# Column maxima of one more batch by GpSimd instead of TensorE, fewer idle products, and a new hand-written order of all pieces

## The chip, the core and the metric

The kernel runs on one core of a Trainium2 chip. The metric is device time in microseconds (us) of one execution, as the median over runs. The engines are PE (TensorE: matrix products and transposes), DVE (VectorE), ACT (ScalarE: functions by table), POOL (GpSimd) and SP (SyncE, which here only issues DMAs, in order). "PEld" is the load of weights into PE, which overlaps its products.

## The reference, cut to what matters

```python
q_s = softmax(q over the 64 elements of a head)       # q, k, v: 8 batches, 8 heads, 576 x 64
k_s = exp(k - max(k over the 576 positions)); k_s /= sum over the positions
kv  = einsum('bhsd,bhse->bhde', k_s, v)
x   = einsum('bhsd,bhde->bhse', q_s, kv)  # then 4608 tokens x 512
h   = x @ w_in                            # 512 -> 2048
g   = softplus(h)
out = g @ w_out                           # 2048 -> 512
```

## The kernel before

The 4608 tokens are nine tiles of 512. A tile's `x` is made from four head pairs h; `h` and `g` are handled in 16 blocks j of 128. Most products run as three fp32r products of a high and a low part (hi·hi, hi·lo, lo·hi; L595 to L597 for the up products, L637 to L639 for the down products), and a 128x512 product of this kind is the unit of nearly all of PE's work. Tiles 0 to 2 are made plainly; tiles 3 to 8 in three pairs by a scheme with seven products in place of eight (L722 to L724, L836 to L838), whose operands are sums of blocks that DVE, ACT and POOL form (L252 to L293, L679 to L686, L803). Weights are decoded and split once in tile 0, stored to DRAM (`keep_w`, L220) and fetched again later (`fetch_w`, L224; `fetch_in`, L230), as are the sums (L265, L293, fetched at L241, L790).

For each batch b and head pair h a "kv unit" of ten pieces makes `kv`: `top` (DVE reduces the five chunks of positions to one maximum for each partition and column, L336), the maximum over the 128 partitions, `shift` (DVE subtracts, L371), `power` (ACT, exp, L377), `product` (PE, L387), and `scale`, `high`, `low`. For the maximum over the partitions there are two ways. Up to batch `ON_PE`, PE transposes the maxima (`turn`, L355), DVE reduces them to a column (`across`, L364) and PE transposes the column, spread to 128 columns, back (`spread`, L367); `shift` reads it from PSUM. Above `ON_PE`, POOL does it in one call (L339) and the pieces 1 to 3 are empty. Batch 0 has a form of its own (L350, L360).

No scheduler orders the work. One string, `ORDER`, names every piece, and `do` issues the pieces one after the other; each engine runs its own instructions in that order, and semaphores hold it where a piece's input isn't there. Tokens: `k2.1.3` is piece 3 of the kv unit of batch 2, head pair 1; `q` softmax of q; `x` a piece of x's making (flip of q, split, product); `T M S J P Q` decoding and splitting of weights; `U A G O` (with 16t+j) up products, softplus, split of g, down products; `D` and `R` stores and fetches; `Y y X C r t e d o` the paired scheme; `n` and `L` loads of k, v and q. `w5.5` issues five idle products of the identity into a bank nobody reads (L1038); they stand at the start, before PE has real work. Batches are 0-based in the code: the "third batch" is b = 2.

Of the kernel before, what the change touches and what calls it, by code (L numbers as in the profile page):

```python
# [1096 lines left out]
```

## Time and profile before

| what | value |
|---|---|
| time, median of 3 runs | 814.32 us (813.33 to 815.51) |
| span of the profiled execution, first to last instruction | 811.1 us |
| median time less this span | 3.2 us |
| PE busy | 800.8 us, 99% of the span |
| DVE, ACT, POOL busy | 625.9, 536.3, 115.1 us |
| granted PE clock | 1.000 |

The profiled execution has no time of its own apart from its span; the 3.2 us between the span and the median are taken as what lies around it. Busy time of PE is counted with overlaps of pipelined products taken once; a 128x512 fp32r product is listed with 0.39 us, but the next one starts 0.23 us after it.

### The profile page before, as it was taken

The numbers are of one execution on the slowest core, as the hardware profiler recorded it, in microseconds if no ns is written. First come the engines' busy times: TensorE is split into PE (matmuls) and PEld (weight loads), VectorE is DVE, ScalarE is ACT, GpSimd is POOL, SyncE is SP. The second block draws the span as 40 slices with busy tenths as digits, with TensorE's granted clock in tenths as the row PEclk, the third lists the DMA queues.
The fourth block names the chain that finished last, engine by engine and source line by source line (L and its number), as shares of the span: only waits on it lengthen the run. The fifth ranks groups of instructions, "written<-read, shape, count | busy, mean of one in ns | idle before, by whom it ended". The sixth has DMA issues, their size and how long they took to land.

```text
span 811.1 us, 12147 instructions
## 1 busy us (share of the span) xinstructions
PE 800.8 (99%) x4244; PEld 656.6 (81%) x4244; DVE 625.9 (77%) x1027; ACT 536.3 (66%) x868; POOL 115.1 (14%) x219
## 2 busy tenths in 40 slices
...
PEclk9999999999999999999999999999999999999999
...
GB/s 340 373 273 182 59 39 274 267 176 385 401 279 257 328 337 343 340 372 253 139 324 237 186 115 265 275 270 93 280 201 197 178 261 198 175 156 322 211 126 70
DMA packets 114493, 193.75 MB, mean 239 GB/s; under 512 B 8000, under 2 KB 90176, under 8 KB 104192
## 3 DMA queue, kind: packets, MB, share of 16 engines
...
q10 hardware_dynamic: 320, 0.26, 0.1%
...
HBM read 149.95 MB, written 42.99 MB: 238 GB/s over the span
## 4 chain that ended last, share of the span: by engine, by line
PE 92%; DVE 3%; issue 2%; DMA 2%; SPq 1%; ACT 0%; POOL 0%; DVEq 0%; ACTq 0%; POOLq 0%
PE po L722 6%; PE po L838 6%; PE po L836 6%; PE po L837 6%; PE po L724 6%; PE po L723 6%; PE ph L595 5%; PE po L637 5%; PE ph L597 5%; PE ph L596 5%; PE po L638 5%; PE po L639 5%; PE ph L722 3%; PE ph L724 3%; PE ph L723 3%; PE ph L836 3%
## 5 line engine op out<-in xcount | busy, mean ns | idle before, releaser
L881 POOL DMA_DIRECT2D out<-w x92 | 59.3, 653 | 305.7 <-DVE w L873 304.4
L816 ACT CAST g_hi<-w 128x512 fp32r<-128x512 f32 x74 | 46.2, 624 | 31.1 <-PE ph L837 8.0
L595 PE MATMUL ph<-x,w 128*128 128x512 f32 x164 | 65.3, 398 | 1.1 <-DMA w<-kept 1.1
L637 PE MATMUL po<-w,g_hi 128*128 128x512 f32 x164 | 64.5, 394 | 0.0
L596 PE MATMUL ph<-x,w 128*128 128x512 f32 x164 | 64.0, 390 | 0.0
L597 PE MATMUL ph<-x,w 128*128 128x512 f32 x164 | 64.0, 390 | 0.0
L639 PE MATMUL po<-w,g_lo 128*128 128x512 f32 x164 | 64.0, 390 | 0.0
L638 PE MATMUL po<-w,g_hi 128*128 128x512 f32 x164 | 63.9, 390 | 0.0
L819 DVE TENSOR_TENSOR g_lo<-w,g_hi 128x512 fp32r<-128x512 f32 x74 | 51.0, 690 | 16.0 <-ACT g_hi L816 12.6
L803 DVE TENSOR_TENSOR w<-w,w 128x512 f32<-128x512 f32 x72 | 49.2, 686 | 5.3 <-ACT w L756 5.2
L752 ACT ACTIVATE w<-w 128x512 f32<-128x512 f32 x48 | 30.1, 632 | 34.8 <-DVE w L745 18.9
L745 DVE TENSOR_TENSOR w<-po,w 128x512 f32<-128x512 f32 x24 | 16.6, 690 | 46.9 <-PE po L724 46.3
L816 ACT CAST w<-w 128x512 fp32r<-128x512 f32 x52 | 32.2, 623 | 25.1 <-DVE w L819 8.1
L604 ACT ACTIVATE g<-ph 128x512 f32<-128x512 f32 x48 | 28.6, 599 | 29.8 <-PE ph L597 26.7
L722 PE MATMUL po<-w,x 128*128 128x512 f32 x112 | 44.1, 394 | 0.0
L724 PE MATMUL po<-w,x 128*128 128x512 f32 x112 | 43.7, 390 | 0.0
L723 PE MATMUL po<-w,x 128*128 128x512 f32 x112 | 43.7, 390 | 0.0
L610 ACT CAST g_hi<-g 128x512 fp32r<-128x512 f32 x46 | 28.6, 621 | 21.2 <-PE po L638 20.7
L613 DVE TENSOR_TENSOR g_lo<-g,g_hi 128x512 fp32r<-128x512 f32 x46 | 31.4, 683 | 12.6 <-ACT g_hi L610 12.4
L339 POOL PARTITION_ALL_REDUCE mx<-mx x20 | 17.2, 860 | 160.6 <-DVE mx L336 133.0
L336 DVE TENSOR_REDUCE mx<-kvt 128x128 f32<-128x640 f32 x28 | 36.9, 1319 | 2.5 <-DMA kvt<-in_kv_tail 2.5
L819 DVE TENSOR_TENSOR w<-w,w 128x512 fp32r<-128x512 f32 x52 | 35.6, 689 | 3.1 <-ACT w L816 1.0
...
## 6 DMA issues: line engine op xcount, KB each, us to landing
...
```

Of the source, the lines that this page charges most:

```text
L595: nc.tensor.matmul(ph, lhsT=w_hi, rhs=x_hi, start=h == 0, stop=False)
L596: nc.tensor.matmul(ph, lhsT=w_lo, rhs=x_hi, start=False, stop=False)
L597: nc.tensor.matmul(ph, lhsT=w_hi, rhs=x_lo, start=False, stop=h == HP - 1)
L637: nc.tensor.matmul(po, lhsT=g_hi[:, ms], rhs=w_hi, start=j == 0, stop=False)
L638: nc.tensor.matmul(po, lhsT=g_hi[:, ms], rhs=w_lo, start=False, stop=False)
L639: nc.tensor.matmul(po, lhsT=g_lo[:, ms], rhs=w_hi, start=False, stop=j == NJ - 1)
L722: nc.tensor.matmul(ph, lhsT=w_hi, rhs=x_hi, start=c == 0 and i in (0, 4), stop=False, **more)
L723: nc.tensor.matmul(ph, lhsT=w_lo, rhs=x_hi, start=False, stop=False, **more)
L724: nc.tensor.matmul(ph, lhsT=w_hi, rhs=x_lo, start=False, stop=c == 1, **more)
L816: nc.scalar.copy(ring[p, i, s][0], right_of(p, i, s))
L819: engine.tensor_tensor(out=lo, in0=right_of(p, i, s), in1=hi.bitcast(F32), op=ALU.subtract)
L836: nc.tensor.matmul(bank, lhsT=w_hi, rhs=hi, start=begin, stop=False, **more)
```

## The change

`ON_PE` goes from 2 to 1, so that the four kv units of batch 2 take their maxima over the partitions from POOL: eight transposes on PE (four L355, four L367) and four short reductions on DVE (L364) go, four calls of L339 come. Of 38 idle products 31 stay, in blocks of 20, 2, 3, 4 and 2 in place of 20, 5, 6 and 7. `ORDER` is written anew from end to end; no other piece is dropped or added (some tokens that did nothing are gone). The functions are the same, 156 lines further down, since the new string is written over many lines. Two ACT table loads fewer follow from the order (48 to 46).

```diff
-ON_PE = 2
+ON_PE = 1
...
 ORDER = """
-    w0.20 b0 b1 q0.0 n k0.0.1 n q0.1 n n q0.2 q0.3 q0.4.1 l0 q0.5 l1 k0.0.2 k0.1.1 l2 k0.1.2 k0.0.3 ...
+    b0 q0.0 b1 q0.1 n n w0.20 k0.0.1 n n q0.2 q0.3 q0.5 q0.4.1 q0.6 k0.0.2 k0.1.1 k0.1.2 k0.0.3 k0.0.4 k0.0.5
+    k0.2.1 k0.2.2 k0.1.3 k0.1.4 w4.2 k0.2.3 k0.2.4 w5.3 k0.1.5 q0.8 l0 k0.3.1 k0.3.2 k0.2.5 k0.0.6 T0 M0.1 w1.2
...
```

**The start, on PE.** Before, the last idle products and the first products of tile 0's x (L558, L583 are its first products of `x` and of `h`):

```order
L480 MATMUL ph_145<-s,pair 128x32
L382 MATMUL att_107<-one,x_192 64x1 x10
L387 MATMUL po_142<-x_192 64x64 x10
L382 MATMUL att_108<-one,x_197 64x1 x10
L387 MATMUL po_143<-x_197 64x64 x10
L1038 MATMUL ph_144<-ident 128x128 x7
L558 MATMUL po_140<-w_137,q_lo 128x512
L558 MATMUL po_141<-w_137,q_lo 128x512
```

After, the same place (156 lines on):

```order
L636 MATMUL ph_145<-s,pair 128x32 x2
L1194 MATMUL ph_144<-ident 128x128 x2
L538 MATMUL att_107<-one,x_192 64x1 x10
L543 MATMUL po_142<-x_192 64x64 x10
L538 MATMUL att_108<-one,x_197 64x1 x10
L543 MATMUL po_143<-x_197 64x64 x10
L714 MATMUL po_141<-w_137,q_lo 128x512
L714 MATMUL po_140<-w_137,q_lo 128x512
```

The seven idle products just ahead of x's first product are gone, two stand further ahead, and x begins with head pair 1 in place of 0.

**Batch 2's transposes, on PE.** Before, amid the down products of tile 0, two of the eight stand here; after, no L511 or L523 (the same two lines) stands behind those of batch 1:

```order
L637 MATMUL po_1387<-w_575,g_hi 128x512
L638 MATMUL po_1387<-w_575,g_hi 128x512
L639 MATMUL po_1387<-w_575,g_lo 128x512
L367 MATMUL att_107<-ident,m_1560 128x128
L355 MATMUL att_108<-ident,mx 128x128
L637 MATMUL po_1384<-w_635,g_hi 128x512
```

**Tile 2's fetches of weights, on SP.** Before, the fetches (L224) for the up products U34 (`w_2120`) and U35 (`w_2180`) stand one pair of loads of k and v (L314, L318) apart:

```order
L265 DMA sums_1963<-w_1682 128x2048
L432 DMA qt<-in_q 128x2048
L224 DMA spare<-kept_1292 128x2048
L265 DMA sums_2037<-w_1711 128x2048
L241 DMA x_2060<-sums_1963 128x2048
L314 DMA kvt<-in_kv 128x8x128
L318 DMA kvt<-in_kv_tail 64x2x128
L224 DMA w_2120<-kept_1309 128x2048
L314 DMA kvt<-in_kv 128x8x128
L318 DMA kvt<-in_kv_tail 64x2x128
L224 DMA w_2180<-kept_1324 128x2048
```

After, with U34's weights in `w_2146` and U35's in `w_2168`:

```order
L421 DMA sums_2046<-w_1248 128x2048
L380 DMA spare<-kept_1586 128x2048
L421 DMA sums_2089<-w_1577 128x2048
L470 DMA kvt<-in_kv 128x8x128
L474 DMA kvt<-in_kv_tail 64x2x128
L380 DMA w_2146<-kept_832 128x2048
L470 DMA kvt<-in_kv 128x8x128
L474 DMA kvt<-in_kv_tail 64x2x128
L380 DMA w_2168<-kept_1075 128x2048
```

The load of q's next tile and the fetch of the sums (L241) stand elsewhere now; the two pairs of loads are still between and ahead of the fetches.

**U34 and U35, on PE.** Before, they follow each other:

```order
L596 MATMUL ph_2205<-x_2054,w_2120 128x512
L597 MATMUL ph_2205<-x_2054,w_2120 128x512
L595 MATMUL ph_2234<-x_1740,w_2180 128x512
L596 MATMUL ph_2234<-x_1740,w_2180 128x512
L597 MATMUL ph_2234<-x_1740,w_2180 128x512
```

After, 24 down products and two groups of products of k and v stand between; the rows at the seam to U35:

```order
L795 MATMUL po_2218<-spare,g_lo 128x512
L543 MATMUL att_107<-kvt 64x65 x10
L543 MATMUL att_108<-kvt 64x65 x10
L751 MATMUL ph_2301<-x_1715,w_2168 128x512
L752 MATMUL ph_2301<-x_1715,w_2168 128x512
```

## Rows read from the trace of the kernel before

**Rows 1.** The page: busy time by engine, granted clock, chain that ended last.
```profile
PE 800.8 (99%) x4244; PEld 656.6 (81%) x4244; DVE 625.9 (77%) x1027; ACT 536.3 (66%) x868; POOL 115.1 (14%) x219
...
PEclk9999999999999999999999999999999999999999
...
PE 92%; DVE 3%; issue 2%; DMA 2%; SPq 1%; ACT 0%; POOL 0%; DVEq 0%; ACTq 0%; POOLq 0%
```

**Rows 2.** Waits of PE: line waited for, total us, times, longest.
```profile
PE ph L595 <- DMA w<-kept: 1.1, 1, 1.1
...
PE att L535 <- DVE q_lo L529: 0.7, 1, 0.7
...
PE att L387 <- issue: 0.4, 1, 0.4
```

**Rows 3.** Busy time in four stretches: window, engines' busy us (count), PEclk, DMA.
```profile
3.00:30.00 27.00, 26.20 (x335) 22.12 (x336) 23.79 (x53) 16.46 (x28) 7.92 (x17) 1.00 1.05 371
30.00:50.00 20.00, 20.00 (x79) 11.09 (x78) 14.51 (x21) 19.91 (x27) 6.07 (x5) 1.00 1.04 388
...
120.00:180.00 60.00, 60.00 (x321) 49.27 (x320) 30.88 (x58) 30.66 (x46) 8.15 (x12) 1.00 0.61 235
...
240.00:280.00 40.00, 39.29 (x241) 32.12 (x238) 39.51 (x71) 27.95 (x48) 4.34 (x15) 1.00 0.85 280
```

**Rows 4.** Timeline of PE around one transpose: start, duration, line, operation.
```profile
127.83 0.27 PE L355 MATMUL att<-ident,mx 128*128 128x128 f32 x1
127.86 0.48 PE L595 MATMUL ph<-x,w 128*128 128x512 f32 x1
128.18 0.39 PE L596 MATMUL ph<-x,w 128*128 128x512 f32 x1
```

**Rows 5.** Timeline of PE and DVE at the start (an fp32 product counts twice).
```profile
2.99 6.07 PE L1038 MATMUL ph<-ident 128*128 128x128 f32 x40 [2.99 <-DVE ident L120]
...
23.77 1.83 PE L1038 MATMUL ph<-ident 128*128 128x128 f32 x14
23.91 1.28 DVE L555 STREAM_TRANSPOSE w<-qt 128x512 f32<-128x512 f32 x2
25.44 3.60 PE L558 MATMUL po<-w,q_lo 128*128 128x512 f32 x8
28.87 1.45 PE L583 MATMUL ph<-x,w 128*128 128x512 f32 x3
```

**Rows 6.** The chain of waits around U35: start, duration, what.
```profile
222.23 2.55 SPq L318
224.82 8.94 DMA w<-kept
...
233.89 0.47 PE ph L595
```

**Rows 7.** Timeline of DVE and PE at 254 us.
```profile
254.39 1.21 DVE L473 TENSOR_REDUCE s<-qt 128x32 f32<-128x1024 f32 x1
255.52 0.68 DVE L529 TENSOR_TENSOR q_lo<-att,q_hi 128x512 fp32r<-128x512 f32 x1
256.25 0.36 PE L535 MATMUL att<-q_hi,kv_hi 128*128 128x192 f32 x1 [0.71 <-DVE q_lo L529]
```

**Rows 8.** POOL's reductions: the line's durations and who waited for them.
```profile
L339 POOL PARTITION_ALL_REDUCE mx<-mx x20: 702/711/1528, 198.0 to 527.5; - x20
...
  DVE kvt L371: 3.8, 6
```

**Rows 9.** One ACT table load and what follows it, timeline of ACT.
```profile
83.37 1.28 ACT L604 ACT_TABLE_LOAD   x1
84.66 0.60 ACT L604 ACTIVATE g<-ph 128x512 f32<-128x512 f32 x1
```

**Rows 10.** The end, timeline of all engines.
```profile
797.94 7.69 POOL L881 DMA_DIRECT2D out<-w  x12 [5.00 <-DVE w L873]
805.74 0.39 PE L838 MATMUL po<-x,spare 128*128 128x512 f32 x1
807.49 1.21 SPq L904 DMA_DIRECT2D out<-w  x2
```

More of the change, by code (lines that the diff above doesn't have):

```diff
@@ new lines @@
+    b0 q0.0 b1 q0.1 n n w0.20 k0.0.1 n n q0.2 q0.3 q0.5 q0.4.1 q0.6 k0.0.2 k0.1.1 k0.1.2 k0.0.3 k0.0.4 k0.0.5
+    k0.2.1 k0.2.2 k0.1.3 k0.1.4 w4.2 k0.2.3 k0.2.4 w5.3 k0.1.5 q0.8 l0 k0.3.1 k0.3.2 k0.2.5 k0.0.6 T0 M0.1 w1.2
+    q0.7 k0.0.7 l1 T1 M1.1 w2.2 k0.3.3 k0.3.4 k0.1.6 k0.3.5 l2 q0.12 k0.1.7 k0.1.8 q0.13 w3.2 q0.9 q0.11.1 q0.10
+    x0.1.0 k0.0.8 l3 n l4 T2 k0.2.6 k0.2.7 k0.2.8 x0.0.0 k0.3.6 k0.3.7 x0.3.0 k0.3.8 x0.1.1 x0.0.1 x0.1.2 x0.2.0
+    J0 k1.0.0 x0.3.1 x0.2.1 x0.0.2 x0.3.2 B0 T3 J1 B1 k1.0.1 x0.2.2 B2 B3 k1.0.2 U0 M2.1 J2 k1.0.3 k1.0.4 n
@@ new lines @@
+    k1.1.0 U1 M3 S3.1 J3 T4 k1.1.1 M4.1 k1.0.5 A0 A1 L1 q1.0 P2 l5.6.7.8.9 k1.0.6 x0.0.3 x0.3.3 Q2 x0.3.4 x0.0.4
+    x0.1.3 x0.1.4 x0.2.3 x0.2.4 P3 Q3 O0 U2 U3 T5 M5 J4 q1.1 T7 k1.1.2 k1.1.3 q1.2 k1.0.7 T6 A2 G2 A3 O1 k1.1.4
+    S5.1 J5 P4 M6.1 Q4 J6 P5 k1.2.0 O2 G3 q1.3 T8 Q5.1 U4 U5 O3 M8.1 M7.1 J7 k1.1.5 k1.1.6 P6 Q6 z1 A4 G4 O4 J8
+    k1.1.7 q1.4 P7 Q7 A5 G5 T11 T10 M10 U6 T9 M9 S10 S9 J9 P8 Q8 A6 G6 U7 A7 O5 D5 U8 q1.5 q1.7 z0 k1.1.8 k1.1.9
+    k1.0.8 k1.0.9 k1.2.1 O6 P9 Q9 D2 k1.2.2 T12 M12.1 k1.3.0 k1.3.1 G7 k1.2.3 q1.6 M11.1 J10 P10 q1.8 J11 O7 A8
@@ new lines @@
+    Q10 T14 P11 Q11 G8 J12 q1.9 U9 W1 U10 A9 U11 T13 P12 A10 A11 O8 G9 O9 M13.1 Q12 D6 k1.3.2 k1.3.3 M14.1
+    k1.2.4 k1.2.5 J13 P13 G10 G11 k1.3.4 Q13 k1.3.5 T15 M15.1 J14 k1.2.6 k1.2.7 k1.2.8 k1.2.9 q1.10 x1.0.0 J15
+    U12 O10 U13 k1.3.6 A12 G12 D3 k1.3.7 x1.0.1 W3 W2 W0 x1.0.2 P14 Q14 O11 O12 x1.0.3 D14 A13 G13 k1.3.8 k1.3.9
+    P15 x1.1.0 x1.1.1 x1.1.2 O13 Q15.1 P0 x1.1.3 q1.11 x1.0.4 x1.0.5 x1.2.0 x1.2.1 U14 U15 x1.2.2 x1.2.3 x1.1.4
+    x1.1.5 A14 G14 x1.3.0 Q0.1 O14 P1 x1.2.4 x1.3.1 x1.3.2 x1.3.3 x1.3.4 k2.0.0 Q1.1 x1.2.5 x1.3.5 Y0.0 k2.1.0
@@ new lines @@
+    k2.1.4 U16 A15 L2 U17 A16 U18 A17 D0 G15 A18 O15 q2.0 k2.0.4 D15 q2.1 q2.2 q2.3 G16 G17 D9 q2.5 q2.7 U19
+    q2.4.1 q2.6 q2.8 O16 G18 O17 k2.0.5 k2.0.6 k2.1.5 q2.9 q2.10 k2.0.7 D8 k2.0.8 k2.0.9 A19 G19 k2.1.6 n k2.2.0
+    O18 U20 U21 A20 A21 U22 U23 k2.2.4 k2.2.5 k2.2.6 O19 k2.1.7 k2.1.8 n k2.3.0 k2.3.4 k2.3.5 q2.11 G20 A22 Y0.1
+    Y1.1 A23 k2.2.7 k2.2.8 D1 Y2.1 Y2.0 Y2.2 O20 U24 U25 Y3.0 G21 Y2.3 Y2.4 k2.1.9 O21 D4 G22 H1.7.0 Y2.5 Y3.1
+    Y0.2 Y0.3 O22 Y0.4 Y0.5 D10 Y0.6 H1.7.1 O23 k2.2.9 x2.0.0 x2.0.1 x2.0.2 x2.0.3 A24 A25 Y3.2 Y3.3 Y1.0 x2.0.4
@@ new lines @@
+    Y3.4 x2.0.5 Y3.5 Y1.2 H1.8.0 H1.9.0 H1.8.1 k2.3.6 k2.3.7 Y2.6 Y4.1 U26 A26 Y2.7 k2.3.8 k2.3.9 O24 H1.9.1 D12
+    O25 n n H1.10.0 x2.1.0 U27 x2.1.1 k3.0.0 x2.1.2 x2.1.3 L3 k3.1.0 Y3.6 q3.1 x2.2.0 H1.10.1 x2.2.1 U28 x2.1.4
+    A27 H1.11.0 Y1.3 Y1.4 Y1.5 A28 O26 H1.12.0 D7 U29 U30 H1.11.1 Y2.8 R0.0 x2.2.2 x2.2.3 x2.1.5 x2.3.0 L4 Y4.0
+    Y7.0 Y4.2 A29 Y7.1 Y4.3 A30 D13 O27 Y6.0 Y3.7 Y3.8 H1.12.1 x2.3.1 Y0.7 k3.0.4 k3.0.5 q3.0 Y6.1 O28 x2.3.2
+    x2.3.3 U31 Y1.6 Y1.7 H1.13.0 H1.13.1 k3.1.4 k3.1.5 H1.14.0 H1.14.1 x2.3.4 x2.3.5 x2.2.4 x2.2.5 q3.12 q3.2
@@ new lines @@
+    q3.4 O29 y0.0 A31 q3.3 H1.15.0 Y0.8 Y7.2 R0.1 k3.0.6 y0.1 y0.2 y0.3 k3.0.7 q3.6 q3.8 q3.5 q3.7 q3.13 q4.0
+    k3.1.6 Y1.8 U32 U33 k3.1.7 A32 O30 H1.15.1 Y4.4 n k3.2.0 R0.2 q3.9 k3.2.4 k3.1.8 n k3.3.0 H2.0.0 q3.11
+    H2.0.1 R0.3 R0.4 O31 F1.0 F1.1 F1.2 k3.1.9 A33 H2.1.0 H2.1.1 q3.10 U34 F1.3 O32 R0.5 y2.0 A34 k3.2.5 H2.2.0
+    k3.3.4 k3.0.8 k3.0.9 q4.1 y1.1 k3.3.5 q4.12 O33 k3.2.6 k3.2.7 H2.2.1 k3.2.8 y1.0 k3.3.6 k3.3.7 k3.3.8 q4.2
+    y0.4 U35 y1.2 q4.4 k3.2.9 y2.1 k3.3.9 y0.5 U36 n A35 H2.3.0 x3.0.0 H2.3.1 q4.6 U37 D11 O34 x3.0.1 q4.3
@@ new lines @@
+    k4.0.0 q4.5 A36 H2.4.0 y0.6 q4.7 x3.0.2 x3.0.3 n x3.1.0 x3.1.1 O35 k4.1.0 q4.8 x3.1.2 x3.1.3 A37 R0.6 U38
+    Y6.2 x3.0.6 x3.2.0 Y7.3 k4.0.4 x3.2.1 k4.1.4 k4.0.5 q4.13 x3.2.2 x3.2.3 x3.1.6 H2.4.1 R0.7 O36 R0.8 x3.2.6
+    x3.3.0 x3.3.1 y0.7 k4.0.6 x3.3.2 Y7.4 y1.3 k4.1.5 k4.0.7 y1.4 x3.3.3 q4.9 q4.11 y1.5 y3.1 A38 H2.5.0 H2.5.1
+    y0.8 k4.0.8 k4.0.9 U39 H2.6.0 H2.6.1 x3.3.6 k4.1.6 k4.1.7 Y4.5 O37 R0.9 n n y1.6 y1.7 A39 H2.7.0 y1.8 y4.0
+    U40 U41 R0.10 Y4.6 Y4.7 Y5.0 Y6.3 Y6.4 Y6.5 Y4.8 k4.2.0 k4.3.0 H2.7.1 k4.1.8 k4.1.9 O38 y3.0 R0.11 A40
@@ new lines @@
+    H2.8.0 Y6.6 H2.8.1 Y6.7 O39 R0.12 O40 y3.2 R0.13 k4.2.4 A41 k4.3.4 H2.9.0 H2.9.1 U42 Y7.5 Y5.2 Y5.1 R2.0
+    k4.3.5 y5.0 Y5.3 Y5.4 y3.3 Y5.5 y3.4 k4.2.5 k4.2.6 k4.3.6 A42 H2.10.0 Y6.8 U43 k4.2.7 k4.2.8 Y5.6 y4.1
+    k4.2.9 X0.1.hB11 q4.10 x4.0.0 k4.3.7 Y7.6 Y7.7 Y7.8 x4.0.1 O41 x4.0.2 k4.3.8 k4.3.9 x4.0.3 x4.1.0 x4.1.1
+    Y5.7 Y5.8 x4.0.6 x4.1.2 U44 x4.2.0 x4.1.3 X0.0.hB11 H2.10.1 x4.2.1 y3.5 X0.0.lB11 x4.1.6 x4.3.0 A43 H2.11.0
+    R0.14 O42 R0.15 x4.2.2 y4.2 x4.2.3 x4.2.6 x4.3.1 X0.1.hB21 X0.0.T1 y5.1 H2.11.1 X0.0.hB22 X0.0.T3 X0.1.lB21
@@ new lines @@
+    A44 x4.3.2 y3.6 y4.3 X0.1.lB11 y3.7 X0.1.T1 X0.0.hT1 y4.4 X0.1.hT1 H2.12.0 U45 O43 y4.5 x4.3.3 X0.0.lB22
+    X0.0.T2 H2.12.1 y4.6 y5.2 y5.3 x4.3.6 X0.0.hB21 X0.0.lB21 X0.0.T4 X0.1.T3 X0.1.hB22 n X0.1.lT1 R3.1.0 A45
+    H2.13.0 X0.1.hT3 U46 A46 O44 U47 y3.8 R3.0.0 R2.1 n X0.1.lB22 y4.7 H2.13.1 y6.0 X0.0.hT2 X0.0.lT2 y4.8 O45
+    X0.1.T2 H2.14.0 H2.14.1 I2.14.0 X0.1.lT3 X0.1.hT2 X0.1.T4 y6.1 X0.0.lT1 R4.1.0 A47 H2.15.0 R4.3.0 H2.15.1
+    I2.14.1 X0.0.hT3 C0.0.0 y7.1 X0.1.hT4 X0.1.lT4 y5.4 y5.5 X0.0.lT3 X0.0.hT4 X0.0.lT4 I2.15.0 C0.0.7 C0.0.2
@@ new lines @@
+    y6.2 X0.1.lT2 y6.3 y6.4 y6.5 R4.0.0 L5 y5.6 y5.7 R3.2.0 L6 C0.0.1 C0.0.8 C0.0.9 y2.2 y2.3 y2.4 I2.15.1 F2.0
+    F2.1 C0.0.3 C0.1.0 F2.2 F2.3 C0.0.4 C0.1.7 k5.0.0 y5.8 C0.1.1 R4.2.0 C0.0.10 C0.0.5 y2.5 C0.0.11 C0.0.6 R2.2
+    C0.1.8 C0.1.3 y2.6 y2.7 y2.8 R4.4.0 C0.1.2 C0.2.0 C0.1.9 y7.0 y7.2 y7.3 y7.4 y7.5 k5.1.0 R3.3.0 C0.1.10 y7.6
+    y7.7 C0.1.4 C0.1.11 C0.0.14 C0.1.5 R2.3 C0.2.7 C0.2.2 C0.2.1 R3.4.0 C0.1.6 k5.0.4 k5.0.5 k5.0.6 R4.5.0 n
+    y6.6 C0.2.8 k5.1.4 k5.1.5 C0.2.9 k5.1.6 C0.0.15 C0.0.16 q5.0 q5.1 q5.12 C0.0.12 C0.2.3 q5.2 C0.2.10 C0.3.0
@@ new lines @@
+    C0.2.4 q5.3 n C0.2.5 R2.4 C0.1.14 C0.3.7 C0.3.1 y6.7 C0.3.2 k5.0.7 k5.1.7 q5.5 k5.1.8 C0.2.11 C0.2.12 C0.3.9
+    y6.8 C0.4.0 C0.2.6 R4.6.0 C0.3.8 C0.3.3 C0.1.15 C0.3.4 R3.5.0 k5.2.0 k5.3.0 C0.2.14 k5.0.8 k5.0.9 C0.3.10
+    C0.3.5 R2.5 k5.2.4 C0.3.11 k5.2.5 C0.3.6 C0.4.7 q5.4 t0.1.0 C0.4.1 k5.3.4 k5.3.5 C0.4.2 R3.6.0 k5.2.6 k5.1.9
+    C0.3.15 q6.0 C0.2.15 C0.4.8 q5.6 q5.7 q5.8 k5.3.6 C0.3.16 k5.2.7 k5.3.7 C0.4.3 q5.13 q5.9 k5.3.8 q5.11
+    C0.4.10 C0.4.4 k5.2.8 C0.3.14 C0.5.0 C0.5.7 C0.5.4 C0.4.11 C0.4.5 C0.4.14 C0.5.2 C0.5.9 e0.0.0.0 C0.5.1
@@ new lines @@
+    t0.1.1 q5.10 k5.2.9 x5.0.0 x5.0.1 x5.0.2 e0.0.0.1 C0.5.8 k5.3.9 C0.4.6 C0.4.9 t0.1.4 e0.0.1.0 e0.0.1.1
+    C0.5.3 C0.5.10 x5.1.0 C0.1.16 C0.5.11 x5.0.3 y7.8 x5.1.1 n x5.1.2 C0.4.15 x5.0.6 C0.6.0 C0.6.7 x5.2.0 n
+    t0.1.3 k6.0.0 k6.1.0 C0.5.5 x5.1.3 C0.1.12 k6.0.4 x5.2.1 R2.6 C0.6.4 C0.6.1 x5.1.6 R3.7.0 C0.4.12 C0.6.8
+    C0.5.6 k6.0.5 C0.6.3 C0.6.10 x5.2.2 C0.7.0 x5.3.0 k6.1.4 k6.1.5 x5.2.3 x5.3.1 C0.6.11 C0.6.5 x5.3.2 C0.5.15
+    C0.5.14 q6.1 x5.2.6 e0.0.3.0 e0.0.3.1 C0.7.7 e0.0.2.0 t0.1.5 e0.0.2.1 q6.12 C0.6.2 x5.3.3 k6.0.6 C0.6.14
@@ new lines @@
+    R2.7 C0.7.1 C0.7.4 q6.2 C0.6.9 q6.3 X1.1.hB11 X1.1.lB11 C0.5.16 C0.6.6 x5.3.6 k6.1.6 C0.7.8 k6.0.7 k6.0.8
+    X1.0.hB11 q6.4 q6.6 q6.5 k6.0.9 r0.0 C0.7.3 C0.7.10 C0.2.16 d0.0.0 n k6.2.0 r0.1 d0.0.1 d0.0.2 q6.8 n R4.7.0
+    C0.7.11 e0.0.4.0 e0.0.5.0 X1.0.lB11 k6.1.7 k6.1.8 t0.1.2 C0.7.5 k6.1.9 r0.2 C0.7.2 r0.3 C0.7.9 e0.0.4.1
+    e0.0.6.0 q6.7 d0.0.3 e0.0.5.1 e0.0.7.0 C0.3.12 d0.0.4 C0.7.6 k6.2.4 e0.0.7.1 d0.0.5 e0.3.0.0 k6.3.0 k6.2.5
+    e0.0.6.1 e0.3.0.1 d0.0.6 d0.0.7 C0.6.12 C0.6.15 d0.3.0 C0.7.15 e0.3.1.0 C0.5.12 k6.2.6 n k6.3.4 k6.3.5
@@ new lines @@
+    k6.3.6 e0.3.3.0 t0.2.0 t0.3.0 r0.4 e0.3.1.1 t0.2.1 e0.3.2.0 k6.2.7 k6.3.7 e0.3.2.1 C0.7.12 e0.3.3.1 t0.1.6
+    d0.3.1 d0.3.2 d0.3.3 e0.3.4.0 e0.3.4.1 d0.3.4 C0.7.14 t0.1.7 e0.3.5.0 e0.3.5.1 t0.2.5 e0.3.7.0 d0.3.5
+    e0.3.7.1 C0.7.16 t0.2.3 e0.3.6.0 e0.3.6.1 d0.3.6 e0.1.0.0 k6.2.8 o0.spread.0 t0.2.4 t0.2.2 t0.3.2 e0.1.0.1
+    t0.2.7 e0.1.1.0 e0.1.1.1 r0.6 t0.3.4 k6.2.9 o0.spread.1 e0.1.2.0 e0.1.2.1 d0.3.7 e0.1.3.0 e0.1.3.1 d0.1.0
+    e0.1.4.0 q6.13 k6.3.8 C0.4.16 t0.3.7 t0.2.6 o0.v.0 d0.1.1 d0.1.2 e0.1.6.0 r0.5 e0.1.5.0 e0.1.4.1 e0.1.5.1
@@ new lines @@
+    e0.1.6.1 d0.1.3 e0.1.7.0 d0.1.4 d0.1.5 e0.1.7.1 t0.3.5 t0.4.5 e0.2.0.0 X1.0.hB21 e0.2.0.1 X1.0.lB21 e0.2.1.0
+    t0.3.6 C0.6.16 d0.1.6 d0.1.7 e0.2.3.0 r0.7 q6.9 e0.2.1.1 d0.2.0 e0.2.2.0 d0.2.1 e0.2.2.1 d0.2.2 e0.2.4.0
+    r0.9 e0.2.4.1 e0.2.3.1 d0.2.3 e0.2.5.0 d0.2.4 e0.2.5.1 d0.2.5 t0.4.2 q6.10 e0.2.6.0 e0.2.6.1 o0.u.0 t0.3.1
+    e0.2.7.0 o0.u.1 d0.2.6 e0.4.0.0 e0.4.1.0 x6.0.0 x6.0.1 e0.4.0.1 e0.2.7.1 d0.2.7 e0.4.2.0 k6.3.9 x6.1.0
+    x6.0.2 x6.0.3 X1.1.hB21 X1.1.lB21 x6.1.1 e0.4.1.1 r0.8 d0.4.0 e0.4.2.1 d0.4.1 d0.4.2 t0.3.3 t0.4.1 q6.11
@@ new lines @@
+    x6.1.2 x6.1.3 o0.v.1 e0.4.3.0 e0.4.3.1 e0.4.4.0 e0.4.4.1 d0.4.3 r0.10 x6.0.6 x6.2.0 e0.4.5.0 n e0.4.5.1
+    e0.4.6.0 d0.4.4 e0.4.6.1 x6.2.1 x6.2.2 x6.2.3 e0.4.7.0 e0.4.7.1 x6.1.6 x6.3.0 x6.3.1 x6.2.6 t0.4.3 e0.5.0.0
+    X1.1.T1 X1.0.T1 e0.5.0.1 X1.0.T3 d0.4.5 X1.0.hB22 d0.4.6 e0.5.2.0 x6.3.2 d0.4.7 e0.5.3.0 X1.0.lB22 o0.c22.0
+    r0.11 e0.5.1.0 o0.c11.0 R3.0.1 x6.3.3 x6.3.6 X1.1.hB22 d0.5.0 e0.5.4.0 t0.4.7 e0.5.1.1 d0.5.1 e0.5.2.1
+    e0.5.3.1 d0.5.2 e0.5.6.0 d0.5.3 e0.5.4.1 d0.5.4 X1.1.lB22 e0.5.5.0 X1.1.T3 X1.1.T2 e0.5.5.1 X1.1.hT2
@@ new lines @@
+    o0.c22.1 X1.1.T4 X1.1.hT4 d0.5.5 o0.c11.1 t0.4.0 e0.5.6.1 e0.6.0.0 e0.6.1.0 X1.1.hT1 R2.8 C1.0.0 X1.1.lT4
+    e0.5.7.0 e0.5.7.1 d0.5.6 d0.5.7 o0.c12.0 o0.flip.3.0 o0.store.3.0 C1.0.7 C1.0.2 e0.6.0.1 e0.6.1.1
+    o0.flip.1.1 e0.6.2.0 e0.6.2.1 r0.12 d0.6.0 d0.6.1 t0.4.4 e0.6.3.0 R3.1.1 e0.6.4.0 X1.0.T2 d0.6.2 X1.0.hT2
+    e0.6.5.0 e0.6.3.1 t0.4.6 d0.6.3 e0.6.6.0 C1.0.9 e0.6.4.1 e0.6.5.1 X1.0.hT3 X1.1.lT1 e0.6.6.1 r0.13
+    o0.store.1.1 d0.6.4 X1.0.hT1 e0.6.7.0 e0.6.7.1 d0.6.5 d0.6.6 X1.0.T4 d0.6.7 e1.0.0.0 X1.0.lT3 X1.1.lT2
@@ new lines @@
+    X1.0.lT2 X1.1.hT3 C1.0.1 o0.c12.1 C1.1.0 o0.flip.3.1 R3.2.1 X1.0.hT4 C1.0.8 X1.0.lT1 R4.0.1 R2.9 o0.c21.0
+    X1.0.lT4 L7 C1.0.3 C1.1.7 o0.flip.0.0 X1.1.lT3 C1.0.4 L8 C1.1.2 k7.0.0 k7.1.0 k7.1.4 C1.0.10 C1.0.5 R4.2.1
+    R2.10 C1.1.1 C1.1.9 R3.3.1 R4.1.1 C1.1.8 o0.c21.1 C1.0.11 C1.0.6 C1.0.15 o0.store.3.1 o0.flip.1.0 k7.1.5
+    C1.1.3 C1.1.10 C1.1.4 C1.2.0 C1.1.5 k7.0.4 o0.flip.2.0 o0.store.2.0 q7.0 k7.0.5 C1.1.11 q7.1 k7.0.6 k7.0.7
+    R2.11 n k7.1.6 n C1.0.14 C1.2.7 C1.2.2 R3.4.1 C1.2.9 C1.2.1 C1.2.8 C1.1.14 k7.1.7 k7.1.8 C1.3.0 C1.2.3
```

68 lines of the change are left out of this document (67 added, 1 removed).

## The prediction

> **What bounds the kernel now.** I read the page first, then the waits of PE, then the stretches, then the timelines at each wait. The page says that PE is the bound: busy for 800.8 of 811.1 us, at the full granted clock in every slice, and 92% of the chain that ended last is PE's [rows 1]. So the change can take off only three things: work that PE does without need, waits of PE, and the way to the first product and from the last one. PE's waits after the start are few: 1.1 us for a fetched weight, 0.7 us for a low part of q, 0.4 us at a group of products of k and v [rows 2]. By the stretches, the other engines are near their limit in places: ACT is busy for 19.91 of 20 us between 30 and 50 us, DVE for 39.51 of 40 between 240 and 280 us, while DVE has 29 us to spare between 120 and 180 us [rows 3]. There a new order can give PE waits that the old one doesn't have, or take some away. That is the frame: a floor some 10 us under the present span, of which most (3.0 us ahead of PE's first product, and about 5.4 us from the start of the last down product at 805.74 to the end) is touched by nothing in the diff [rows 1, 5, 10].
>
> **Batch 2's maxima on POOL.** Eight transposes leave PE. One is priced by its neighbours: L355 starts at 127.83, the product behind it at 127.86 and the next at 128.18 [rows 4]. From 127.83 to 128.18 are 0.35 us, where one product alone takes 0.23 (the pace of neighbours in the same stretch), so a transpose costs 0.12 us and not the 0.27 of its record. 8 × 0.12 = **0.9 us less**. These eight stood between 120 and 182 us, where PE has no wait [rows 3], so their time comes off in full. Bounds: nothing, if a wait takes their place; 8 × 0.27 = 2.2 us, if the record were the price.
>
> In their place stand four calls on POOL, of 0.7 to 1.5 us each [rows 8]: 3 to 6 us more on an engine busy for 115 of 811 us. DVE waited for 20 such calls six times, 3.8 us in total [rows 8]; four more would be 4/20 of that, 0.8 us of DVE's time, against four short reductions (L364) that DVE is rid of. Where batch 2's units run, DVE has slack, so I cost this at nothing for PE. What hides it is that slack; without it the 0.8 us would reach PE once at most. [...]
>
> **The start.** Before, the first product of x (L558) starts at 25.44, just as the block of seven idle products ends that began at 23.77; its first input, the first of two flips on DVE that began together at 23.91 and took 1.28 us, was there at about 24.6 [rows 5]. So idle products, not the data, held the first product for up to 0.8 us. After, this block is gone, and the flip of head pair 1 stands ahead of other small pieces of DVE. I added up the durations of the pieces in the new order, engine by engine, each starting when its input and its engine are free: first product of x near 24.1, first product of h near 28.0 (28.87 before [rows 5]), first down product 0.6 to 0.9 us earlier. I take **0.8 us less**. Bounds: nothing, since ACT has no idle time in the 20 us that follow [rows 3], and its amount of work, not its starting point, may set when tile 0's later blocks are ready; and 1.7 us, the length of the removed block [rows 5].
>
> Two ACT table loads go, of 1.28 us each, and the next ACTIVATE starts at once behind a load (83.37 + 1.28 = 84.65 [rows 9]). That is 2.6 us off ACT, part of it in the very stretch where ACT has none to spare; I count it as what lets the start's gain last, and not a second time. [...]
>
> **The waits in the middle.** (1) U35 waits for its weights. SP issued the fetch at 224.82, right behind an issue of 2.55 us for a load of k and v; it landed 8.94 us later, and PE's first product followed at 233.89 [rows 6], 1.1 us late [rows 2]. In the new order the fetch stands at the same place on SP, behind the same two pairs of loads, but 24 down products and two groups of products of k and v stand between U34 and U35: 24 × 0.23 = 5.5 us more room, against 1.1 us missing. This wait should go: **−1.1**. But U34's own fetch, the one before it, now is the tighter one: following SP's queue, it has about 9.2 us, and it needs the 8.9 us that U35's took. (2) L535 waits 0.7 us for q_lo, because DVE runs a reduction of 1.21 us (L473) ahead of it, and q_lo then starts at 255.52 [rows 7]. In the new order the same reduction, and one more of 1.3 us for k ahead of it, stand before that q_lo, while DVE's lead there is about as before: **0**, between −0.7 and +1.3. (3) The 0.4 us at L387 [rows 2] falls with the place of that group: **−0.4**. Bounds of the three together: −2.2 to +1.3 us.
>
> Against this stand new waits. I summed, for both orders, the work that DVE and ACT must have done before each PE piece. DVE's lead is greater in the new order by some 2 to 3 us between 200 and 320 us and at 440 to 490 us, since work was drawn into the idle stretch of 120 to 180 us [rows 3]; from 600 us on by 4 to 10 us. But in tile 0, from 30 to 95 us, DVE's and ACT's margins are 2 to 5 us smaller than before, at some places 0 to 1 us. Since the order is new throughout, I allow **+0.3 us** of new small waits. Bounds: 0 (the old order has three), and 4 us (the whole of the narrowest margins).
>
> **The end.** PE's last product is followed by the way of the last 256 columns to DRAM by SP; before, POOL's stores end at 805.6 and are covered [rows 10]. After, one block of output (a copy, a flip, then four DMAs of 0.64 us each on POOL) is stored later, by my count to within about 1 us of the end. Taken as 0; 1 us if the cover is gone.
>
> **The sum**, against the profiled span: −0.9 (transposes) −0.8 (start) −1.1 −0.4 (waits) +0.3 (new waits) = −2.9 us; 811.1 − 2.9 = 808.2, and with the 3.2 us around it, by which the median of the runs shown exceeds the span, **811.4 us**. A measurement of this kernel tells a change from none at about 0.3%, 2.4 us: faster is below 811.9, slower above 816.8.
>
> **Rivals.** *A* is the forecast, 809.3 to 812.5: chance 0.46. *B, new waits eat the gain:* in tile 0, ACT and DVE run at their limit [rows 3], and each piece that comes 0.3 to 1 us late passes to PE at once. For it: the smaller margins there, and that the removed waits are only 1.5 us. Against: two table loads less on ACT. At the bound of 4 us of new waits the sum is −3.2 + 4, about +1: 812.5 to 816; chance 0.24. *C, slower: SP's in-order queue.* Ahead of U34's fetch stand a store of sums (L421), which waits for its sum, and loads of k and v, which wait for a buffer. If one of them comes late, the fetch and all behind it are late too, and PE pays one for one once U34's room falls under the 8.9 us that such a fetch takes [rows 6]; with 9.2 us of room it pays from 0.3 us late. Slower than now by 2.4 us it is from about 6 us late: 816.8 to 820; chance 0.11. Against it: no such wait of more than 1.1 us occurs in the old order [rows 2]. *D, a larger gain:* the leads in the saturated stretches let PE run without waits from 100 us on, and the start's gain reaches 1.7 us: −0.9 −1.7 −2.2 = −4.8, 809.5; and a further few us if short stalls too small to be listed go as well, down to 804; chance 0.15. [...] That the transposes don't go is no case.
>
> **How the numbers follow.** Faster: D, and A but for 0.08 of it above 811.9: 0.53. Same: B and that part of A: 0.32. Slower: C and E: 0.15. The range of 8 in 10 leaves out about half of D below, and most of C and E above: 807.5 to 816.0.
>
> **What would show it.** Right: no transpose between 110 and 185 us and 24 calls on POOL; x's first product near 24 us; U35 without a wait; PE's waits beyond the start near 1 us in total. Wrong: waits of PE on ACT or DVE between 40 and 100 us (B); a wait for fetched weights at U34 or behind (C); x's eight records longer than 3.6 us (E); an end later than 5.4 us after the last down product's start.

## The result, and the profile after

The changed kernel takes **822.75 us** (median), the kernel before 813.83 us in the same runs: ratio 1.0107 (95% interval 1.0091 to 1.0122). One of its four runs took 1151.2 us, at a granted clock of 0.654; the ratio leaves it out, and the median of the other three is 822.62 us. The forecast was 811.4 us, range 807.5 to 816.0. It is slower, and by none of the rivals as they were told.

The page of the changed kernel, in the order of [rows 1]:

```profile
PE 803.7 (98%) x4222; PEld 655.8 (80%) x4222; DVE 625.2 (76%) x1023; ACT 522.6 (64%) x866; POOL 115.9 (14%) x223
...
PEclk9999998999999999999999999999999999999999
...
PE 86%; DVE 5%; ACT 3%; DMA 2%; issue 2%; POOL 0%; SPq 0%; DVEq 0%; ACTq 0%; POOLq 0%
```

The span is 820.8 us, 9.7 more; PE's busy time grew by 3 only. One slice of the clock is not full. PE's waits, against [rows 2]:

```profile
PE ph L752 <- POOL w L363: 6.9, 1, 6.9
PE ph L1194 <- DVE ident L276: 3.0, 1, 3.0
PE po L795 <- DVE g_lo L769: 1.3, 3, 0.7
PE ph L878 <- DMA x<-sums: 0.5, 1, 0.5
PE po L1052 <- DVE w L1045: 0.5, 1, 0.5
PE po L523 <- DVE m L520: 0.3, 1, 0.3
PE att L691 <- DVE q_lo L685: 0.2, 1, 0.2
PE att L543 <- issue: 0.2, 1, 0.2
```

U35's wait for weights is gone, as forecast; the one at the products of k and v, which was to go too, is halved. One new wait of 6.9 us stands against them: the second product of U17, which needs the low part of weight 1, made on POOL (L363, the line that was L207). POOL's timeline there:

```profile
114.28 2.44 POOL L363 TENSOR_TENSOR w<-w,w 128x1024 fp32r<-128x1024 f32 x1 [1.25 <-ACT w L361]
125.11 0.72 POOL L495 PARTITION_ALL_REDUCE mx<-mx  x1 [8.39 <-DVE mx L492]
133.01 2.38 POOL L363 TENSOR_TENSOR w<-w,w 128x1024 fp32r<-128x1024 f32 x1 [7.17 <-issue]
141.34 0.72 POOL L495 PARTITION_ALL_REDUCE mx<-mx  x1 [5.95 <-issue]
149.24 2.00 POOL L623 TENSOR_TENSOR qt<-qt,m 128x1024 f32<-128x1024 f32 x1 [7.17 <-DVE qt L623]
...
163.93 0.72 POOL L495 PARTITION_ALL_REDUCE mx<-mx  x1 [7.63 <-DMA kvt<-in_kv_tail]
```

The first of batch 2's maxima (L495, the line that was L339) ends at 125.83. The low part, whose high part ACT had ready near 120.6, begins 7.17 us later, and the profile has no reason but "issue". The same gap stands ahead of L623, whose input (L620) was there at 147.59, 1.65 us before it started; on the way back to L495 it is 5.95 us. In the row for L363 stand two instructions that the old kernel doesn't have between these operations, and who waited; the row for L495 has six more:

```profile
L363 POOL TENSOR_TENSOR w<-w,w x4: 2385/2436/2489, 52.6 to 133.0; 128x1024 fp32r<-128x1024 f32 x4
...
L363 POOLq MODIFY_POOL_CONFIG  x2: 98/98/98, 125.8 to 125.8; - x2
...
  DVE w L408: 8.5, 1
  PEld ph L752: 7.3, 1
  PE ph L752: 6.9, 1
...
L495 POOLq MODIFY_POOL_CONFIG  x6: 1/17/18, 116.9 to 156.5; - x6
```

So where POOL goes here from the maximum over partitions to ordinary arithmetic or back, MODIFY_POOL_CONFIG records and a gap stand between, called the change-over below: the records show 0.1 us at 125.8, and the first operation behind them comes 7.2 us later. DVE stood too, 8.5 us, since its next operation (L408) reads the same low part. What PE did then (first column start, second duration):

```profile
128.16 0.39 PE L751 MATMUL ph<-x,w 128*128 128x512 f32 x1
135.44 0.79 PE L752 MATMUL ph<-x,w 128*128 128x512 f32 x1 [6.89 <-POOL w L363]
136.04 0.63 PE L753 MATMUL ph<-x,w 128*128 128x512 f32 x1
136.46 0.63 PE L751 MATMUL ph<-x,w 128*128 128x512 f32 x1
...
138.17 0.60 PE L752 MATMUL ph<-x,w 128*128 128x512 f32 x1
138.60 0.41 PE L753 MATMUL ph<-x,w 128*128 128x512 f32 x1
138.84 0.39 PE L751 MATMUL ph<-x,w 128*128 128x512 f32 x1
```

After the stall the products start 0.43 us apart, not 0.23, until 138.6. The windows (granted clock is the third number from the end) show a granted clock of 0.94 of full in the second stretch and of 0.50 in the next:

```profile
128.00:130.00 2.00, 0.55 (x3) 0.13 (x1) 0.00 (x0) 0.60 (x1) 0.00 (x0) 1.00 0.36 147
130.00:132.00 2.00, 0.00 (x0) 0.00 (x0) 0.00 (x0) 0.00 (x0) 0.00 (x0) 0.94 0.00 0
132.00:134.00 2.00, 0.00 (x0) 0.00 (x0) 0.00 (x0) 0.00 (x0) 0.99 (x1) 0.50 0.00 0
...
138.00:140.00 2.00, 2.00 (x9) 1.54 (x9) 0.00 (x0) 0.20 (x1) 0.00 (x0) 0.85 0.00 0
```

### The profile page after: what moved, and what is told of

It reads as the page before. It is cut to its first block, busy times and chain, and to the rows that moved or that the text cites. A ratio compares the mean times of both kernels' runs of the same rounds, so it can differ in the third digit from the quotient of the medians.

```text
span 820.8 us, 12003 instructions
## 1 busy us (share of the span) xinstructions
PE 803.7 (98%) x4222; PEld 655.8 (80%) x4222; DVE 625.2 (76%) x1023; ACT 522.6 (64%) x866; POOL 115.9 (14%) x223
## 4 chain that ended last, share of the span: by engine, by line
PE 86%; DVE 5%; ACT 3%; DMA 2%; issue 2%; POOL 0%; SPq 0%; DVEq 0%; ACTq 0%; POOLq 0%
PE po L992 7%; PE po L994 7%; PE po L993 7%; PE po L878 5%; PE po L880 5%; PE po L879 5%; PE po L793 4%; PE po L795 4%; PE po L794 4%; PE ph L751 4%; PE ph L752 4%; PE ph L753 4%; PE ph L878 3%; PE ph L879 3%; PE ph L880 3%; PE ph L994 2%
## 5 line engine op out<-in xcount | busy, mean ns | idle before, releaser
L769 DVE TENSOR_TENSOR g_lo<-g,g_hi 128x512 fp32r<-128x512 f32 x46 | 34.6, 755 | 15.5 <-ACT g_hi L766 15.4
L495 POOL PARTITION_ALL_REDUCE mx<-mx x24 | 19.0, 792 | 178.0 <-DVE mx L492 162.4
L752 PEld LDWEIGHTS ph<-x,w 128*128 128x128 f32 x164 | 31.2, 190 | 13.4 <-POOL w L363 7.3
```

Source lines behind the costliest of these rows:

```text
L752: nc.tensor.matmul(ph, lhsT=w_lo, rhs=x_hi, start=False, stop=False)
```

## The experiments

Theory S: the whole loss is POOL's change-over, with PE and DVE queued behind it. Rival O: the new order as a whole is worse. The time of before beside each run is that of the same runs, 813.1 to 813.8 us. All times are medians in us:

| run | time | ratio to before (95%) |
|---|---|---|
| e1_swap | 813.84 | 1.0009 (0.9998 to 1.0021) |
| e2_no_switch | 812.9 | 0.9989 (0.9976 to 1.0003) |
| e3_new_order_pe | 824.75 | 1.0138 (1.0122 to 1.0155) |
| e4_old_order_pool | 816.44 | 1.0035 (1.0024 to 1.0047) |
| e5_filled | 822.54 | 1.0111 (1.0094 to 1.0128) |
| e6_transposes | 812.41 | 0.9986 (0.9976 to 0.9997) |
| e7_tail | 812.1 | 0.9994 (0.9979 to 1.0009) |
| e8_idle14 | 813.49 | 1.0006 (0.9996 to 1.0016) |
| e9_no_block | 813.05 | 0.9992 (0.9983 to 1.0) |
| e10_tail_no_switch | 812.75 | 0.9992 (0.9982 to 1.0001) |

**e1_swap**, one swap in the changed kernel's order:

```diff
-k2.0.0 Q1.1
+Q1.1 k2.0.0
```

> The changed kernel with one swap of two neighbours in the order: the low part of weight 1 (on POOL, L363) is issued ahead of the first maximum of batch 2 (POOL, L495), not behind it. Theory S (POOL needs about 7.2 us to go from L495 back to an ordinary operation, and PE stood 6.9 us because L363 stood behind L495): the wait at 128 us goes, and with it the stretch at the lower clock behind it; 812 to 814.5 us, some 9 us less than the changed kernel. L363 then starts as soon as its high part is there, near 120.7 us. The two other goings to and fro of POOL stay, about 6 to 7 us each, and nobody waits for them. Rival O (the order as a whole made the inputs of that operation late, or POOL's issue is slow for another reason): 821 to 824 us, the wait moves with L363.

813.84 us, as S has it: 8.9 us less for two tokens. POOL's timeline now:

```profile
119.89 2.43 POOL L363 TENSOR_TENSOR w<-w,w 128x1024 fp32r<-128x1024 f32 x1 [3.85 <-ACT w L361]
130.92 1.53 POOL L495 PARTITION_ALL_REDUCE mx<-mx  x2 [8.61 <-issue]
139.68 1.93 POOL L623 TENSOR_TENSOR qt<-qt,m 128x1024 f32<-128x1024 f32 x1 [7.23 <-DVE qt L623]
```

The low part starts at once. The change-over ahead of the first L495 takes 8.61 us here, more than the 5.95 of the changed kernel, and the one ahead of L623 still 7.23 us. PE's list of waits has no row on POOL: it costs only where PE needs what stands behind it.

**e2_no_switch**, POOL's last two ordinary operations on DVE:

```diff
-k2.0.0 Q1.1
+k2.0.0 Q1
...
-q2.4.1
+q2.4
```

> The changed kernel with the low part of weight 1 and the one half of the third tile's softmax shift (L623) on DVE in place of POOL, so that POOL does no ordinary arithmetic once it has done its first L495. Theory S: no wait of 7 us on POOL anywhere, no configuration of POOL after the first; 812 to 814.5 us, within 1 us of the swap, since DVE has room between 120 and 180 us for 2.4 us more. Rival O: 820 us or more, with PE waiting at the same product, for DVE now.

812.9 us; no configuration stands between POOL's operations after the first (two records at L495, at 116.7 and 116.8 us, and none behind them). The 2.4 us more on DVE are hidden, as expected.

**e3_new_order_pe**, batch 2 on TensorE in the new order (excerpt):

```diff
-ON_PE = 1
+ON_PE = 2
...
-k2.1.0 k2.1.4 U16 A15 L2 U17 A16 U18 A17
+k2.1.0 U16 k2.0.1 k2.1.1 A15 L2 U17 k2.0.2 k2.1.2 A16 U18 k2.0.3 k2.1.3 k2.1.4 A17
```

> The new order with batch 2's maxima on TensorE again (the limit at 2, pieces 1 to 3 of the four units put between the products, and one low part of k and v moved ahead). Theory S: POOL's first L495 comes only with batch 3, after POOL's last ordinary arithmetic; no wait on POOL; 812.5 to 815.5 us, the swap's time plus 0.9 us for eight transposes. Rival O (the order itself costs the time): 819 to 823 us.

824.75 us, against S at first sight. But PE has no wait on POOL here; its waits are of another kind:

```profile
PE po L791 <- ACT g_hi L764: 3.5, 1, 3.5
PE po L793 <- DVE g_lo L767: 3.2, 3, 1.9
```

My places for the pieces are at fault: the shift of a unit stands on DVE ahead of splits of g, and waits there for a transpose that PE does later (L525 waits 4.81 us for L521 at 178 us). At both waits the granted clock fell too, to 0.53 in 144 to 146 us and 0.50 in 182 to 184 (0.994 over the whole execution). The run tells nothing of the order itself, and rests as inconclusive.

**e4_old_order_pool**, only the limit changed in the old order:

```diff
-ON_PE = 2
+ON_PE = 1
```

> The old order with batch 2's maxima on POOL (only the limit is changed, 2 to 1). Theory S: the second of these calls ends near 112 us and three low parts of weights stand right behind it on POOL; with 7.2 us between, the first starts near 119.2 and ends near 121.7, where PE wants it at 118.9: a wait of about 2.7 us, less 0.9 us for the transposes: 814.5 to 817.5 us. Rival O (the move to POOL costs nothing, only the new order does): 812.5 to 813.5 us, the old time less 0.9.

816.44 us, inside S's 814.5 to 817.5. The change-over stands elsewhere and is paid there, at the product and the time that was worked out from the old trace:

```profile
111.67 0.70 POOL L339 PARTITION_ALL_REDUCE mx<-mx  x1 [16.90 <-DVE mx L336]
119.28 2.39 POOL L207 TENSOR_TENSOR w<-w,w 128x1024 fp32r<-128x1024 f32 x1 [6.91 <-issue]
```

```profile
118.92 0.40 PE L595 MATMUL ph<-x,w 128*128 128x512 f32 x1
121.72 0.50 PE L596 MATMUL ph<-x,w 128*128 128x512 f32 x1 [2.40 <-POOL w L207]
```

The new order is not needed for the loss. Together with e1, where two tokens take the whole loss back and the rest of the new order stays, this rules rival O out as its cause.

**e5_filled**, the changed kernel with idle products in the gap:

```diff
-U16 A15 L2 U17
+U16 w9.28 A15 L2 U17
...
-nc.tensor.matmul(warm[:, 0:P], lhsT=ident, rhs=ident, start=True, stop=True)
+nc.tensor.matmul((banks[0] if at[0] == 9 else warm)[:, 0:P], lhsT=ident, rhs=ident, start=True, stop=True)
```

> The changed kernel with 28 idle products (into a bank that is free there) between the up products of U16 and U17, so that PE is busy while U17's low part is late. 28 products of 0.22 us fill 6.3 of the 7.3 us. If the clock behind the stall is a cost of its own: the products that follow start 0.23 us apart from the first on, not 0.43 as seven of them did; 1.4 us less than the changed kernel: 821 to 822 us. If it is not (the later waits for DVE set the time anyway): 822.5 to 823.5 us. The end of the stall itself, which POOL sets, should not move.

822.54 us: no difference that can be told. With the idle products in the gap (127.77 to 133.38), the products behind it start 0.23 us apart (134.53 to 139.81); what was won there was lost 5 us later:

```profile
139.81 0.39 PE L794 MATMUL po<-w,g_hi 128*128 128x512 f32 x1
142.37 0.50 PE L795 MATMUL po<-w,g_lo 128*128 128x512 f32 x1 [2.18 <-DVE g_lo L769]
```

In the changed kernel that wait is at most 0.7 us. DVE had stood behind the same low part, then behind a second change-over of 6.00 us, and its delay sets the time. And behind this wait the clock fell after all:

```profile
142.00:144.00 2.00, 1.63 (x6) 1.35 (x7) 2.00 (x3) 1.49 (x3) 0.00 (x0) 0.87 0.00 0
144.00:146.00 2.00, 2.00 (x6) 1.52 (x6) 1.93 (x6) 0.80 (x2) 0.00 (x0) 0.50 0.72 266
```

The products from 143.77 to 146.33 us start 0.43 us apart. So the run moved the stretch at the lower clock by some 12 us and didn't remove it; whether that stretch is a cost on top of the stall stays open.

**e6_transposes**, the old order, batch 2 on POOL, with the first pieces behind POOL's last ordinary operation:

```diff
-ON_PE = 2
+ON_PE = 1
...
-Q10 k2.0.0 P11
+Q10 P11
...
-G13 k2.1.0 M15.1
+G13 M15.1
...
-q2.4.1 A16
+q2.4.1 k2.0.0 k2.1.0 A16
```

> The old order with batch 2's maxima on POOL, and the first pieces of its first two head pairs moved behind POOL's last ordinary operation, so that POOL changes over once, with nobody waiting. What the transposes alone are worth: 8 x 0.12 = 0.9 us less than before by the prediction, 812.4 to 813.3 us, no wait of PE on POOL. If the calls cost something elsewhere (waits of DVE that reach PE): 813.5 to 815 us.

812.41 us, 0.95 us less than before (813.36). From U2's first product to the last down product are 804.63 − 40.34 = 764.29 us, before 805.74 − 40.60 = 765.14: 0.85 us, the eight transposes near the price of [rows 4]. The change-over is there, but PE has no wait on POOL; DVE waits for the first call, 2.52 us:

```profile
136.77 2.14 POOL L339 PARTITION_ALL_REDUCE mx<-mx  x2 [6.41 <-issue]
```

Against e4, which differs only in where the first pieces of two units stand, this is 4.0 us less.

**e7_tail**, the swap (not shown again) and the last store by POOL where it stood in the old order (excerpt):

```diff
-d2.6.2.1 d2.6.3.1 o2.store.3.1 d2.6.5.0 d2.6.6.0 t2.4.7 e2.6.7.0 e2.6.7.1 d2.6.7.0 d2.6.4.1 d2.6.5.1 o2.c21.0 o2.flip.2.0
+o2.store.3.1 d2.6.5.0 d2.6.6.0 t2.4.7 e2.6.7.0 e2.6.7.1 d2.6.7.0 o2.c21.0 o2.flip.2.0 d2.6.2.1 d2.6.3.1 o2.store.2.0 d2.6.4.1 d2.6.5.1
...
-o2.storep.1 o2.store.2.0
+o2.storep.1
```

> The swap, and at the end the last store by POOL back to where it stood in the old order (four half products of the last step later, the store four products before the end). If the four stores by POOL, issued in the last 7 us, are what makes SP's last two stores land in 2.8 us and not in 1.9 as before: landing 1.9 us again, about 0.9 us less than the swap, 812.5 to 813.3 us. If not: as the swap, 813.5 to 814 us.

812.1 us. Landing of SP's last two stores, first in the swap, then here (from issue, least, median and most):

```profile
DMA to landing us min/median/max: 2.7/2.8/2.9
```

```profile
DMA to landing us min/median/max: 1.9/1.9/1.9
```

The landing answers as expected: POOL's last store is issued 0.4 us ahead of SP's two in the swap (806.2 and 806.6 us), 1.9 us ahead here (805.1 and 807.0). The time (1.7 us less than the swap's, in other runs) lies below both ranges that were expected; its interval overlaps the swap's, so the 0.9 us aren't told apart from noise.

**e8_idle14** and **e9_no_block**, idle products taken away, from the swap and from e6:

```diff
-w0.20
+w0.14
...
-S0 w2.3 k0.1.7 w3.2 k0.2.7
+S0 k0.1.7 k0.2.7
-x0.0.0 w4.2 x0.0.1
+x0.0.0 x0.0.1
```

> The swap with a first block of 14 idle products in place of 20. If that block holds up the first transposes of k (in the new order x's first product follows the first of them by 15.0 us in three profiles): the first one starts near 9.0 us and not at 9.7 to 10.5, and the time is 0.5 to 1.5 us less than the swap's, 812.3 to 813.3 us. If the loads or the softmax of q set it, or the lower clock then lasts longer: no change, 813.4 to 814.5 us.

> The old order with the transposes moved to POOL without a change-over in anyone's way, and without the seven idle products just ahead of x's first product. By the prediction's term for the start (idle products hold x's first product for up to 0.8 us): x's first product starts 15.6 - 0.8 = 14.8 us behind the end of PE's first idle block's successor, the first transpose, in place of 15.6 to 16.5; 0.5 to 0.9 us less than with them, 811.5 to 812 us against before at 813.4. If ACT and DVE set the pace of tile 0 whatever the first product does: no difference, 812.2 to 812.8 us, with new waits of PE before 50 us.

813.49 and 813.05 us: no gain in either; e9 lies above both ranges that were expected. In e8 PE's first transpose starts at 7.83 us, but the next one waits for its load, and x's first product starts at 24.38, within the spread of the new order's other profiles (24.23 to 25.47). In e9 the first product of x starts 14.95 us after the first transpose of k; in e6, which differs from e9 by the seven idle products alone, 25.17 − 9.53 = 15.64. So it comes 0.7 us sooner, as the prediction's term for the start has it. But PE now stands 0.90 us for the flip, and the clock falls:

```profile
24.79 5.31 PE L558 MATMUL po<-w,q_lo 128*128 128x512 f32 x8 [0.90 <-DVE w L555]
...
24.00:26.00 2.00, 1.21 (x2) 0.72 (x3) 1.97 (x6) 1.92 (x5) 1.94 (x6) 0.67 1.07 330
26.00:28.00 2.00, 2.00 (x3) 0.79 (x3) 2.00 (x4) 1.44 (x4) 0.40 (x3) 0.50 1.04 351
```

The eight products of x take 5.31 us, before 3.60 [rows 5], and U2 starts at 41.66, later than before (40.60). This is what rival E stood for, a lower clock at the start, but in the old order: the 0.7 us that the idle products held up, and more (5.31 − 3.60 = 1.7 us), was lost at the lower clock when they were gone.

**e10_tail_no_switch**, e2's and e7's edits together.

> The new order with the old place of the last store and with POOL's last two ordinary operations on DVE: both mended at once. If the two add up (change-over: nothing left to gain against the swap but waits behind it, up to 0.9 us; tail: 0.9 us): 811 to 812 us, less than either kernel. If the rest of the new order's waits are what is left: 812 to 813 us. By either, within 0.3% of before: the new order without the change-over is worth about 1 to 2 us.

812.75 us: by its interval not told from before. The two don't add up to a time below either alone.

## Why the prediction was wrong

**The step that failed** is "I cost this at nothing for PE", on the four calls of POOL. It counted their durations (0.7 to 1.5 us) and looked for who waits for their results, and there it was right: in e2, where the change-over is out of the way, DVE waits 3.8 us for the 24 calls, as for the 20 of before [rows 8]. It didn't count what the calls do to the operations behind them on POOL: between such a call and ordinary arithmetic lie 6.8 to 7.2 us (after, e1, e4, e5), and the other way 6.0 to 8.6 (after, e5, e6, e1), the call's input having been ready 4 us or more before. The old kernel makes this change once, between POOL's last ordinary arithmetic and batch 3's first call, where nobody waits:

```profile
127.69 2.96 POOL L467 TENSOR_TENSOR qt<-qt,m 128x1024 f32<-128x1024 f32 x1 [0.99 <-DVE m L464]
...
197.98 0.72 POOL L339 PARTITION_ALL_REDUCE mx<-mx  x1 [9.71 <-DVE g_lo L613]
...
L339 POOLq MODIFY_POOL_CONFIG  x2: 15/15/15, 188.4 to 188.5; - x2
```

With batch 2 on POOL the first call comes before POOL's last ordinary operations, and the new order puts weight 1's low part right behind it. The traces count it: two configuring instructions on POOL before, ten after (two each at L363 and L623, six at L495). The price in PE's time: 135.44 − 128.16 − 0.23 = 7.05 us of stall, 7 × 0.20 = 1.4 us of products at the lower clock, and the remaining 0.9 us of waits behind it: between U2's start and the last down product the changed kernel takes 774.61 us (814.97 − 40.36), the swap 765.30 (804.91 − 39.61), 9.3 us less. How the last two share their part isn't settled: in e5 the same stretch takes 775.00 us. e1 and e2 show the cause by removing it, e4 by making it in the old kernel, e6 by moving it there to where PE doesn't need what stands behind it.

Why a change-over takes this long isn't shown: the configuring instructions show 0.1 us or less, and for the rest of the 6.0 to 8.6 us the profile names nothing but "issue" or an input that was there earlier.

**The other terms.** *Transposes, −0.9:* right; −0.85 in e6. *The start, −0.8:* right in size as a mean. U2's first product starts at 40.60, 40.81 and 40.34 us in the old order (before, e4, e6), and at 40.36, 39.61, 40.23, 39.12 and 39.74 in the new one (after, e1, e2, e7, e10): means 40.58 and 39.81. In the profile of the changed kernel itself x's first product comes no earlier than before (25.47 and 25.44), since PE's first transposes start at 10.46 there and at 8.98 before. Counted from them, U2 starts 30.8 to 31.6 us later in the old order and 29.9 to 30.2 in the new one. The reason, idle products that hold x's first product, is borne out by e9 (0.7 us sooner without them), where the granted clock then fell to 0.50 (26 to 28 us) and U2 came no sooner (41.66). *U35's wait, −1.1, and the products of k and v, −0.4:* the first is gone, the second halved, and in e2 and e10 a wait of 0.6 us on ACT stands at such a group. *q_lo, 0:* waits of 0.2 to 0.9 us in total stay. *New waits, +0.3:* too small. From U2 to the last down product the mended versions of the new order (e1, e2, e7, e10) take 765.30, 766.46, 766.11 and 764.93 us, mean 765.7, against the forecast's 765.14 − 0.9 − 1.5 + 0.3 = 763.0: 2.7 us more. PE's lists of waits show little of it: their rows between these points sum to 1.6 us in e1 and 2.2 us before, where the forecast took off 1.2. The rest lies in gaps too short to be listed, and where it comes from stays open. *The end, 0:* from the start of the last down product to the end are 5.88, 6.18 and 5.87 us (after, e1, e2), before 5.40: 0.5 to 0.8 us too little. The cover was not gone, but with POOL's four stores later SP's last two land later (e7: 5.31).

So without the change-over the change is worth nothing that can be told (e1, 1.0009), and the 2.4 us between the forecast and e1 went to small gaps and to the end. That is rival B's outcome; its mechanism, waits on ACT or DVE in tile 0, isn't shown. Rivals C and E didn't occur in the changed kernel: its granted clock read 0.50 at the stall (132 to 138 us) and 1.00 at the start of x (24 to 28 us), where e9 read 0.67 and 0.50. No run shows the clock levels and the loss behind E's part of the chances (0.15 with C's 0.11); the runs showed in their place a granted clock of 0.50 of full, and in e9 5.31 us for the eight records of x in place of 3.60 [rows 5]. The 3.2 us around the span were mis-sized too: in the changed kernel each time lies 1.8 us above its own span, before 2.0 to 2.1; the 3.2 came from setting the median of three runs against one span.
